# Spreading a row maximum over the partitions: by nine TensorE transposes, or by one and a trip through DRAM

## The chip, the core and the metric

The kernel runs on one core of a Trainium2 chip. The metric is the device time of one execution in microseconds (us). The engines are named as in the profile: PE is TensorE (PEld its weight loads), DVE VectorE, ACT ScalarE, POOL GpSimd, SP SyncE, which here only issues DMAs. L213 is line 213 of the kernel before.

## What is computed

Attention (batch 2, 8 heads, 576 positions, head size 64, rotary embedding) gives 1152 tokens of 512 numbers. A first mixture of 8 experts follows, weighted by a normalised table, and then a second mixture, in which every token goes to exactly one expert and no expert takes more than 144:

```python
N, D = x.shape                       # 1152, 512
E = w_gate.shape[1]                  # 8
cap = N // E                         # 144
logits = x @ w_gate
flat = logits.flatten()
order = np.argsort(-flat)
assigned = -np.ones(N, dtype=np.int64)
counts = np.zeros(E, dtype=np.int64)
for idx in order:
    tok, e = (int(idx) // E, int(idx) % E)
    if assigned[tok] >= 0 or counts[e] >= cap:
        continue
    assigned[tok] = e
    counts[e] += 1
out = np.zeros((N, D), dtype=np.float32)
for e in range(E):
    mask = assigned == e
    h = np.maximum(x[mask] @ w1[e], 0.0)
    out[mask] = h @ w2[e]
```

## The kernel before

Everything ahead of the second mixture is the same in both kernels. The second mixture (`moe2`) replaces the sorted walk by eight **phases**, each of which fills one expert. Tokens lie as 9 tiles of 128 partitions.

**A phase p**, p = 0 to 6. `prefer` (L205, L206) masks the experts that are full and takes each token's best logit, m, a [128, 9] tile. To compare every token with every other, each partition needs all 1152 best logits: the tile `mb`, [128, 9, 128]. `bcast` (L213) makes it with PE, nine transposes of one column of m spread over 128 columns, in three PSUM banks, and `bcopy` (L216) copies each bank to SBUF on ACT. `onehot` (L221 to L226) marks each token's best expert. `compare` on DVE (L245 to L248) and `above` on ACT (L237, L239) fill nine tables `cmp`, one for each tile j of the other token; ACT takes part of tables 5 to 8. `count` (L256) multiplies the tables with the marks on PE, in three groups of 27 matmuls, so that each token learns how many better ones want its expert. `assign`, `total`, `close` and `left` (L264 to L297) settle who is placed and which expert is now full.

Then expert p's tokens are collected: `select` and `place` (L309 to L319), `spread` (L326, L328), `index` (18 matmuls, L342), `address` (L348, L350), and `gather` (L360), two indirect DMAs on POOL's queue (xa, xb: 72 rows of ysc each), which end with a memset of `tick` (L364). ysc is the DRAM copy of the tokens; `save` (L1039) writes it tile by tile from SP, the last from ACT. `weights` loads the expert's weights on SP: four DMAs of 512 KB (`wlo`, L380) after a register load of the expert's number, and four (`whi`, L384) after a load of `tick`, that is, after the gather has been issued. Phase 7 needs no comparison.

**An expert p** turns the gathered rows (`tin`, L445 and L446; for expert 0 `turn` and `join`, L455 and L461, which add the part that never went to DRAM), runs 32 products into h (L471, ACT relu L474) and 32 into y (L481, ACT copy L484), turns y back (`tout`, L490, ACT L491) and scatters it (L496). Each product is two matmuls on the chip.

**What sets the order.** Phases and experts, and the last products of the first mixture (L769), are handed to `Plan`. It keeps a list of operations with what each needs and estimated durations per engine, and repeatedly emits the one that could start first; the products form its main line. Each engine then runs its instructions in that order. `HOLD` makes a phase's comparisons from table HOLD[p] on wait, on DVE, for the tick of the gather before (`hold`, L336): in phase 1 from table 1 on, in phase 2 from table 0 on. `mb`, `m` and the other phase tiles have two buffers; the PSUM bank PV has one.

Of the kernel before, what the change touches and what calls it, by code (L numbers as in the profile page):

```python
# [21 lines left out]
F32 = mybir.dt.float32  # L22
# [3 lines left out]
AF = mybir.ActivationFunctionType  # L26
# [5 lines left out]
N, D, E, F = 1152, 512, 8, 1024  # L32
# [3 lines left out]
NT = N // 128  # L36
# [6 lines left out]
@with_exitstack  # L43
def tile_attention_moe_moe2(
    ctx: ExitStack,
    tc: tile.TileContext,
    q: bass.AP,
    k: bass.AP,
    v: bass.AP,
    wg1: bass.AP,  # L50
    w1: bass.AP,
    w2: bass.AP,
    wg2t: bass.AP,
    w1b: bass.AP,
    w2b: bass.AP,
    rope: bass.AP,
    rt: bass.AP,
    out: bass.AP,
    dbg=None,
):  # L60
    nc = tc.nc
    ctx.enter_context(tc.manual_schedule())
    consts = ctx.enter_context(tc.tile_pool(name="consts", bufs=1))
    lp = ctx.enter_context(tc.tile_pool(name="big", bufs=1, side="right"))
    xst = ExitStack()
    xp = xst.enter_context(tc.tile_pool(name="xp", bufs=1, side="right"))

    ident = consts.tile([128, 128], F32, name="ident")
    make_identity(nc, ident)

    xH = xp.tile([128, KT, N], F32R, name="xH")
    xL = xp.tile([128, KT, N], F32R, name="xL")

    lg = consts.tile([128, NT, E], F32, name="lg")
    dram = ctx.enter_context(tc.tile_pool(name="dram", bufs=1, space=bass.MemoryType.DRAM))
    ysc = dram.tile([N + 1, D], F32, name="ysc")
    ps = ctx.enter_context(tc.tile_pool(name="ps", bufs=2, space=PSUM))
    sst = ExitStack()
    pss = sst.enter_context(tc.tile_pool(name="pss", bufs=2, space=PSUM))
    if dbg is not None and "xT" in dbg:  # L80
        with xst, sst:
            attention(tc, nc, ps, pss, lp, q, k, v, rope, ident, xH, xL, None)
            nc.sync.dma_start(dbg["xT"][0], xH.bitcast(F32))
            nc.sync.dma_start(dbg["xT"][1], xL.bitcast(F32))
        return
    m1 = Moe1(tc, nc, ctx, ps, sst, lp, wg1, w1, w2, wg2t, rt, ident, xH, xL, lg, ysc)
    attention(tc, nc, ps, pss, lp, q, k, v, rope, ident, xH, xL, m1)
    m1.rest()
    if dbg is not None and "acc" in dbg:
        m1.dbg = dbg["acc"]  # L90
        nc.sync.dma_start(dbg["lg"], lg)
    xst.close()
    moe2(tc, nc, ctx, ps, m1, w1b, w2b, ident, lg, ysc, out)


TINY = 2.0 ** -120
# [67 lines left out]


CFG = dict(CG=3, NCMP=6, HA=20, LEAD=8, FILL=0)
JA = 5
MAIN, HOLD, AT = 0.715, {1: 1, 2: 0}, (33, 34)


def moe2(tc, nc, ctx, ps, m1, w1b, w2b, ident, lg, ysc, out):
    BIG = 3.0e38
    FAR = 1.0e6
    if True:
        two = ctx.enter_context(tc.tile_pool(name="m2b", bufs=2, side="right"))
# [13 lines left out]
        def tb(x):  # L189
            return x.unsqueeze(1).to_broadcast([128, NT, E])  # L190
# [3 lines left out]
        def phase(p):  # L194
            d = {}
            S_[p] = d
            last = p == E - 1

            def prefer():
                lm = two.tile([128, NT, E], F32, name="lm") if p else None  # L200
                m = two.tile([128, NT], F32, name="m")
                if p == 0:
                    lm = lg
                else:
                    V.tensor_tensor(lm, lg, tb(pen), op=OP.add)  # L205
                V.tensor_reduce(m, lm, axis=AX.X, op=OP.max)  # L206
                d["lm"], d["m"] = lm, m
                d["mb"] = two.tile([128, NT, 128], F32, name="mb")

            def bcast(c):  # L210
                d["pm", c] = pm = ps.tile([128, 512], F32, name="T", bufs=3)[:, 0:384].rearrange("p (t c) -> p t c", t=3)
                for t in range(3):
                    nc.tensor.transpose(pm[:, t], d["m"][:, c * 3 + t:c * 3 + t + 1].to_broadcast([128, 128]), ident)  # L213
# [27 lines left out]
            def compare(j):  # L241
                g = table(j)
                mj = d["m"][:, j:j + 1]
                if 0 < j < JA:
                    V.tensor_scalar(g[:, :j], d["mb"][:, :j], mj, None, op0=OP.is_lt)  # L245
# [142 lines left out]
            def op(name, deps, segs, f, *a):  # L388
                plan.add((name, p), [x if isinstance(x, tuple) else (x, p) for x in deps], segs,
                         lambda: f(*a))  # L390

            if not last:
                op("m", [("close", p - 1), ("left", p - 1)] + ([("at", p)] if p == 1 else []) if p else [("fold", 1)], [("DVE", 0.5, 0.15)], prefer)
                for c in range(3):
                    op(f"bc{c}", ["m"], [("PE", 0.33, 0.2)], bcast, c)
                    op(f"mb{c}", [f"bc{c}"], [("ACT", 0.37, 0.1)], bcopy, c)
                op("oh", ["m"] + ([("ad", p - 1)] if p in HOLD else []), [("DVE", 1.35, 0.1)], onehot)
                mb = ["mb0", "mb1", "mb2"]
                for j in range(JA, NT):
                    op(f"sg{j}", mb[:(j - 1) // 3 + 1], [("ACT", 0.19 + 0.107 * j, 0.1)], above, j, 0)  # L400
                    op(f"re{j}", [f"sg{j}"], [("ACT", 0.1 + 0.107 * j, 0.1)], above, j, 1)
                for j in range(NT):
                    op(f"cmp{j}", mb + (["hold"] if j >= HOLD.get(p, NT) else []), [("DVE", 1.06 if j < JA else 0.88 - 0.067 * (j - 1), 0.15)], compare, j)
                cg = CFG["CG"]
                if p in HOLD:
                    op("hold", [("ga", p - 1)], [("DVE", 0.1, 0.1)], hold)
                js = [list(range(j, min(j + cg, NT))) for j in range(0, NT, cg)]
                for n, g in enumerate(js):
                    op(f"cnt{n}", ["oh"] + [f"cmp{j}" for j in g] + [f"re{j}" for j in g if j >= JA] + (["cnt0"] if n else [("add1", 0)] if p == 1 else []),
                       [("PE", 0.23 * len(g), 0.2)], count, g)  # L410
                op("as", [f"cnt{n}" for n in range(len(js))], [("DVE", 0.8, 0.1)], assign)
                op("tot", ["as"], [("PE", 0.04, 0.2)], total)
                op("left", ["as"], [("DVE", 0.4, 0.1)], left)
                op("close", ["tot"], [("DVE", 1.1, 0.1)], close)
                op("sel", ["close", "left"], [("DVE", 0.6, 0.1)], select)
            else:
                op("sel", [("sel", p - 1), ("left", p - 1)], [("DVE", 1.3, 0.1)], select)
            op("wlo", ["sel" if last else "close"] + ([("yend", p - 3)] if p > 2 else []) + ([("whi", p - 1)] if p else []) + ([("t", 35)] if p == 1 else []),
               [("SP", 0.3, 0), ("DMA", 7.0 if p else 3.5, 2.0)], weights, 0, 4 if p else 2)
            op("pl", ["sel"], [("PE", 0.2, 0.2)], place)  # L420
            op("spr", ["pl"], [("DVE", 1.65, 0.1)], spread)
# [105 lines left out]
        for n, (f, save) in enumerate(m1.tail()):  # L527
# [10 lines left out]
            elif save:  # L538
                t, evac = save
# [13 lines left out]
        for p in range(E):  # L553
            phase(p)
            expert(p)
# [1066 lines left out]
```

## Time and profile before

| | us |
|---|---|
| median of three runs | 1123.04 (1122.49 to 1125.29) |
| the profiled execution | 1122.86 |
| its span, first to last instruction | 1121.1 |
| PE busy in the span | 1102.6 (98%) |
| DVE, POOL, ACT busy | 745.7, 438.6, 412.8 |

The second mixture's phases begin at about 917 us of the span and end at 1044; experts 0 to 3 run beside them, experts 4 to 7 after. Busy time is read by stretch, since the stages have different limits; a wait is read from the idle time of an engine and from what ended it.

### The profile page before, as it was taken

How to read it: one execution, taken by the hardware profiler on the slowest of the kernel's cores; microseconds unless marked ns; L12 is line 12 of the kernel's file. 1: busy time of each engine (PE TensorE's matmuls, PEld its weight loads, DVE VectorE, ACT ScalarE, POOL GpSimd, SP SyncE). 2: the span in 40 equal slices, each digit the busy share in tenths (PEclk: the TensorE clock that was granted, in tenths of full speed). 3: DMA queues.
4: the chain of work that ended last, by engine and by line, in shares of the span. 5: the costliest groups of instructions: out<-in, count | busy, mean ns of one | idle time of the engine just before them, and what ended most of it. 6: DMA issues, size and time to landing. Idle time of an engine off the chain costs nothing.

```text
span 1121.1 us, 20946 instructions
## 1 busy us (share of the span) xinstructions
PE 1102.6 (98%) x8171; PEld 962.0 (86%) x8171; DVE 745.7 (67%) x1688; ACT 412.8 (37%) x903; POOL 438.6 (39%) x449
## 2 busy tenths in 40 slices
PE   7999999999999999999999999999999999999997
PEld 4666678998888888888888889989889888999997
DVE  5777733564777777777777777666678887778200
ACT  5777742143223223222223223232331133566222
POOL 6778353065434335434334534345310000234211
PEclk8999999999999999999999999999999999999999
DMA  5332322001233222432322422112130004879920
GB/s 130 79 74 51 99 82 76 1 1 57 82 98 94 85 86 88 125 98 75 95 85 75 126 92 66 38 39 74 39 141 11 30 1 165 277 250 354 292 75 22
DMA packets 105458, 107.22 MB, mean 96 GB/s; under 512 B 35600, under 2 KB 68752, under 8 KB 105232
## 3 DMA queue, kind: packets, MB, share of 16 engines
q1 hardware_dynamic: 102528, 100.40, 28.6%
q0 software_dynamic: 2048, 4.72, 1.4%
q8 instruction: 64, 1.05, 0.4%
q10 hardware_dynamic: 784, 0.77, 0.2%
q14 instruction: 34, 0.28, 0.1%
HBM read 98.85 MB, written 4.72 MB: 92 GB/s over the span
## 4 chain that ended last, share of the span: by engine, by line
PE 88%; DVE 3%; DMA 3%; issue 2%; ACT 2%; POOL 1%; SPq 1%; POOLq 0%; DVEq 0%; ACTq 0%
PE Y L1001 23%; PE T L939 21%; PE T L750 9%; PE Y L769 8%; PE Y L471 5%; PE Y L481 5%; PE T L1454 3%; PE S L1415 3%; PE T L1382 3%; DMA fr<-in_moe_w 2%; PE T L256 1%; DVE acc L1003 1%; PE PV L1382 1%; DVE v L952 1%; PE PV L1454 1%
## 5 line engine op out<-in xcount | busy, mean ns | idle before, releaser
L939 PE MATMUL T<-xH,wa 128*128 128x256 f32 (+1 forms) x576 | 137.8, 294 | 0.9 <-ACT v L959 0.8
L939 PEld LDWEIGHTS T<-big,wb 128*128 128x128 f32 x864 | 125.7, 188 | 10.8 <-DVE v L952 1.8
L939 PE MATMUL T<-big,wb 128*128 128x256 f32 (+1 forms) x864 | 133.0, 296 | 0.0
L952 DVE TENSOR_TENSOR v<-T,v 128x256 f32<-128x256 f32 (+1 forms) x240 | 108.1, 450 | 37.4 <-PE T L939 34.5
L1003 DVE SCALAR_TENSOR_TENSOR acc<-Y,pw,acc 128x512 f32<-128x512 f32 x168 | 122.5, 742 | 1.5 <-PE Y L1001 0.4
L939 PEld LDWEIGHTS T<-xH,wa 128*128 128x128 f32 x576 | 100.0, 188 | 9.5 <-ACT v L959 3.8
L750 PE MATMUL T<-xH,wa 128*128 128x384 f32 x336 | 92.9, 337 | 0.0
L848 POOL TENSOR_TENSOR wa<-wraw,wa 128x512 fp32r<-128x512 f32 (+1 forms) x48 | 48.8, 1018 | 106.3 <-ACT wa L847 106.3
L945 ACT ACTIVATE hhA<-v 128x256 fp32r<-128x256 f32 x72 | 30.1, 418 | 149.3 <-DVE v L952 149.3
L939 PE MATMUL T<-xL,wa 128*128 128x256 f32 (+1 forms) x288 | 84.5, 293 | 0.0
L945 ACT ACTIVATE hhB<-v 128x320 fp32r<-128x320 f32 x72 | 34.0, 472 | 136.5 <-DVE v L952 136.5
L946 DVE SCALAR_TENSOR_TENSOR hlB<-v,hhB 128x320 fp32r<-128x320 f32 x72 | 57.0, 792 | 38.7 <-ACT hhB L945 38.7
L1001 PE MATMUL Y<-wa,hhB 128*128 128x512 f32 x240 | 75.2, 395 | 0.0
L1001 PE MATMUL Y<-wb,hhB 128*128 128x512 f32 x240 | 75.2, 395 | 0.0
L1073 DVE SCALAR_TENSOR_TENSOR fr<-fr,fc 128x512 f32<-128x512 f32 x64 | 52.5, 820 | 33.6 <-DMA fr<-in_moe_w 33.6
L946 DVE SCALAR_TENSOR_TENSOR hlA<-v,hhA 128x256 fp32r<-128x256 f32 x72 | 51.1, 709 | 35.3 <-ACT hhA L945 35.3
L867 POOL TENSOR_TENSOR wb<-wraw,wb 128x512 fp32r<-128x512 f32 x24 | 30.6, 1299 | 101.9 <-ACT wb L866 101.9
L867 POOL TENSOR_TENSOR wa<-wraw,wa 128x512 fp32r<-128x512 f32 x24 | 30.6, 1294 | 99.1 <-ACT wa L866 99.1
L769 PE MATMUL Y<-wb,hh 128*128 128x512 f32 x216 | 68.4, 398 | 0.0
L750 PEld LDWEIGHTS T<-xH,wa 128*128 128x128 f32 x336 | 61.3, 188 | 2.9 <-issue 0.9
L1424 DVE TENSOR_REDUCE negmax<-S 128x1 f32<-128x576 f32 x72 | 53.8, 748 | 15.0 <-PE S L1415 14.1
L1001 PE MATMUL Y<-wa,hhA 128*128 128x512 f32 x192 | 59.9, 393 | 0.0
(343 smaller groups left out, 2729.1 us busy)
## 6 DMA issues: line engine op xcount, KB each, us to landing
wraw<-in_moe_w SPq DMA_DIRECT2D x52, 512.0 KB, 5.4
fr<-in_moe_w SPq DMA_DIRECT2D x64, 256.0 KB, 5.1
wraw<-in_moe_w SPq DMA_DIRECT2D x48, 256.0 KB, 3.2
big<-in_moe_w SPq DMA_DIRECT2D x20, 512.0 KB, 7.9
wa<-in_moe_w SPq DMA_DIRECT2D x18, 512.0 KB, 5.2
wb<-in_moe_w SPq DMA_DIRECT2D x14, 512.0 KB, 7.6
fc<-in_moe_w_gate SPq DMA_DIRECT2D x9, 256.0 KB, 3.5
t1q<-t1q SPq DMA_DIRECT2D x14, 160.0 KB, 2.8
```

The lines of the kernel that those rows point to most:

```text
L471: nc.tensor.matmul(Z["ph"][:, f % 2], d["wa"][kt // 2][:, kt % 2, f * 128:(f + 1) * 128], Z["xg", p][:, kt], start=(kt == 0), stop=(kt == ...
L481: nc.tensor.matmul(Z["py"][:, b % 2], d["wb"][f // 4][:, f % 4, b * 128:(b + 1) * 128], Z["h", p][:, f], start=(f == 0), stop=(f == FB - 1))
L750: nc.tensor.matmul(p[:, :CH], w[:, wi, kt, (fb % 2) * 128:(fb % 2) * 128 + 128], x[:, kt, o], start=(n == 0), stop=(n == 11))
L769: nc.tensor.matmul(self.Y[c][t], a[:, o], w[:, wi, fb % 2], start=(fb == 0 and n == 0), stop=(fb == FB - 1 and n == 2))
L867: G.tensor_tensor(d["W"][:, 1, h], r[:, 2 + h], d["W"][:, 0, h].bitcast(F32), op=OP.subtract)
L939: nc.tensor.matmul(bank[:, 0:n], d[t][:, ww, b, r * 128:(r + 1) * 128], x(xw, r), start=(first and i == 0), stop=(i == 5), skip_group_chec ...
L945: A.activation(HH[:, f, o], src, AF.Relu)
L946: V.scalar_tensor_tensor(HL[:, f, o], src, 0.0, HH[:, f, o].bitcast(F32), op0=OP.max, op1=OP.subtract)
L952: V.tensor_tensor(o, bank[:, 0:n], x, op=OP.add)
L1001: nc.tensor.matmul(y, h[:, f, o], w[:, ww, f], start=(f == 0 and z == 0), stop=(f == 1 and z == 2))
L1003: V.scalar_tensor_tensor(self.at(t), y, self.pw[:, t, e:e + 1], self.at(t), op0=OP.mult, op1=OP.add)
L1424: V.tensor_reduce(m[0:n], SS[P, i][0:n, :, :288], axis=AX.XY, op=OP.max, negate=True)
```

## The change

From phase 1 on (`VIA = 1`) the nine transposes and three copies go. Instead `turn_m` transposes the whole m at once into a [9, 128] tile (PE, into the bank PV) and copies it to SBUF (ACT), `send_m` writes its 4.6 KB to a DRAM tile from ACT's queue, and `spread_m` reads them back from SP's queue into every partition of mb (576 KB). The plan gets a time for each, `HOLD[1]` goes from 1 to 0, and `wlo` of phases 1 to 5 is made to come after `spread_m` of the next phase.

```diff
-    moe2(tc, nc, ctx, ps, m1, w1b, w2b, ident, lg, ysc, out)
+    moe2(tc, nc, ctx, ps, m1, w1b, w2b, ident, lg, ysc, dram, out)
...
-JA = 5
-MAIN, HOLD, AT = 0.715, {1: 1, 2: 0}, (33, 34)
+JA, VIA = 5, 1
+MAIN, HOLD, AT = 0.715, {1: 0, 2: 0}, (33, 34)
...
+            def turn_m():
+                pt = ps.tile([128, 512], F32, name="PV", bufs=1)[0:NT, 0:128]
+                nc.tensor.transpose(pt, d["m"], ident)
+                d["mt"] = two.tile([NT, 128], F32, name="mt")
+                nc.scalar.activation(d["mt"], pt, AF.Copy)
+
+            def send_m():
+                d["mr"] = dram.tile([NT, 128], F32, name=f"mr{p}")
+                nc.scalar.dma_start(d["mr"], d["mt"])
+
+            def spread_m():
+                nc.sync.dma_start(d["mb"].rearrange("p t c -> p (t c)"),
+                                  d["mr"].rearrange("t c -> (t c)").partition_broadcast(128))
...
-                for c in range(3):
-                    op(f"bc{c}", ["m"], [("PE", 0.33, 0.2)], bcast, c)
-                    op(f"mb{c}", [f"bc{c}"], [("ACT", 0.37, 0.1)], bcopy, c)
+                if p < VIA:
+                    for c in range(3):
+                        op(f"bc{c}", ["m"], [("PE", 0.33, 0.2)], bcast, c)
+                        op(f"mb{c}", [f"bc{c}"], [("ACT", 0.37, 0.1)], bcopy, c)
+                else:
+                    op("ms", ["m"], [("PE", 0.12, 0.2), ("ACT", 0.25, 0.1)], turn_m)
+                    op("mw", ["ms"], [("ACT", 0.06, 0.0)], send_m)
+                    op("ml", ["mw"], [("NONE", 0.0, 2.2)], lambda: None)
+                    op("mi", ["ml"], [("SP", 0.1, 0.0)], spread_m)
+                    for c in range(3):
+                        op(f"mb{c}", ["mi"], [("NONE", 0.0, 3.4)], lambda: None)
...
-            op("wlo", ["sel" if last else "close"] + ([("yend", p - 3)] if p > 2 else []) + ([("whi", p - 1)] if p else []) + ([("t", 35)] if p == 1 else []),
+            op("wlo", ["sel" if last else "close"] + ([("yend", p - 3)] if p > 2 else []) + ([("whi", p - 1)] if p else []) + ([("t", 35)] if p == 1 else []) + ([("mi", p + 1)] if max(VIA - 1, 1) <= p < E - 2 else []),
```

The lines of `moe2` move by 14, and from the list of a phase's operations on by 22: bcast L213 becomes L227, the new transpose is L212, its copy L214, the write L218, the read L221, index L356, h L493 and y L503.

On PE, the turn of m in a later phase. Before, in phase 4, it falls among expert 2's products y (h, wb and wraw are their operands), behind the last matmul of `place`:

```order
L319 MATMUL PV<-selb,ones_b 128x1
L481 MATMUL Y<-h,wb 128x144
L481 MATMUL Y<-h,wraw 128x144
L213 MATMUL T<-ident,m 128x128 x9
L481 MATMUL Y<-h,wraw 128x144 x2
```

In the changed kernel it falls among an expert's products h (xg and wb are their operands), and so in each of phases 3 to 6:

```order
L333 MATMUL PV<-selb,ones_b 128x1
L493 MATMUL Y<-xg,wb 128x144 x2
L212 MATMUL PV<-ident,m 9x128
L493 MATMUL Y<-xg,wb 128x144 x6
L356 LDWEIGHTS hot
```

Nine transposes became one, and the phase stands later against the experts; counted on in the same order, 39 products and the index lie between this turn and the first counts, and 64 products, the three count groups and expert transposes between it and the next turn.

On ACT, in phase 5. Before, three copies fill mb and the comparisons follow at once:

```order
L474 ACTIVATE h<-Y 128x288 x3
L216 ACTIVATE mb<-T 128x384 x3
L237 ACTIVATE cmp_11279<-mb,m 128x640
L237 ACTIVATE cmp_11282<-mb,m 128x768
L474 ACTIVATE h<-Y 128x288
```

Now:

```order
L496 ACTIVATE h<-Y 128x288
L214 ACTIVATE mt<-PV 9x128
L496 ACTIVATE h<-Y 128x288
L218 DMA mr_11305<-mt 9x128
L496 ACTIVATE h<-Y 128x288 x2
L251 ACTIVATE cmp_11386<-mb,m 128x640
```

One relu of h stands between the copy of the turned row and the issue of its write, and two more ahead of the first comparison.

On SP, between the last weight loads of one expert (`whi`) and the first of the next (`wlo`); the ISA rows set registers. Before:

```order
L384 DMA wb<-in_moe_w 128x2x512
L384 ISA
L384 DMA wb<-in_moe_w 128x2x512
L368 TENSOR_LOAD ei
L368 ISA x2
L380 ISA
L380 DMA wb<-in_moe_w 128x2x512
```

Now:

```order
L398 DMA wb<-in_moe_w 128x2x512
L398 ISA
L398 DMA wb<-in_moe_w 128x2x512
L221 DMA mb<-mr_10605 128x1152
L382 TENSOR_LOAD ei
L382 ISA x2
L394 ISA
L394 DMA wb<-in_moe_w 128x2x512
```

The read of mb for phase 3, which waits for the write of the row, now stands ahead of the register load and of expert 2's first four weight loads.

## Rows read from the trace of the kernel before

**Rows 1.** The page, parts 1 and 2: busy time; PE's granted clock in tenths.

```profile
PE 1102.6 (98%) x8171; PEld 962.0 (86%) x8171; DVE 745.7 (67%) x1688; ACT 412.8 (37%) x903; POOL 438.6 (39%) x449
...
PEclk8999999999999999999999999999999999999999
```

**Rows 2.** Stretches: length, busy PE, PEld, DVE, ACT, POOL; PEclk, DMA share, GB/s.

```profile
960.00:970.00 10.00, 10.00 (x128) 9.93 (x128) 7.35 (x23) 6.01 (x9) 1.48 (x3) 1.00 0.99 326
1030.00:1040.00 10.00, 10.00 (x148) 9.88 (x145) 7.22 (x38) 4.08 (x7) 5.06 (x3) 1.00 0.94 314
```

**Rows 3.** Chain that ended last, in order of time: start, us, engine, tile, line, count.

```profile
956.33 0.98 PE T L213 x9
...
958.05 0.60 PE PV L342 x18
...
974.86 0.44 PE Y L490 x4
...
982.25 0.66 PE T L256 x27
...
1047.48 6.13 PE Y L471 x50
```

**Rows 4.** Timeline of PE at the first gather: start, us, instruction, [idle before <-releaser].

```profile
944.67 0.87 PE L769 MATMUL Y<-big,wraw 128*128 128x512 f32 x3
945.69 1.11 PE L455 MATMUL Y<-ident,xa 72*128 72x72 f32 x8 [0.15 <-DMA xa<-ysc,ix]
```

**Rows 5.** Timelines of SP's queue and of POOL, same columns: seventh ysc write, first gather.

```profile
935.96 0.40 SPq L1039 DMA_DIRECT2D ysc<-acc  x1
...
942.34 1.15 POOL L360 DMA_INDIRECT xa<-ysc,ix  x1 [10.30 <-ACT cmp L237]
```

**Rows 6.** DMA issues by window or whole span: count, KB each, us to landing.

```profile
ysc<-acc SPq DMA_DIRECT2D x1, 256.0 KB, 5.2
...
ysc<-pen SPq DMA_DIRECT2D x1, 2.0 KB, 2.2
...
ysc<-acl SPq DMA_DIRECT2D x1, 256.0 KB, 2.0
ysc<-acl ACTq DMA_DIRECT2D x1, 256.0 KB, 5.5
...
wa<-in_moe_w SPq DMA_DIRECT2D x1, 512.0 KB, 3.8
...
fc<-in_moe_w_gate SPq DMA_DIRECT2D x9, 256.0 KB, 3.5
...
g<-in_moe_w_gate SPq DMA_DIRECT2D x1, 2048.0 KB, 7.5
...
big<-in_moe_w SPq DMA_DIRECT2D x1, 512.0 KB, 9.3
```

**Rows 7.** Timeline of DVE, columns as in rows 4: the tick, comparisons of phase 3.

```profile
944.87 0.14 DVE L336 COPY rest<-tick 1x1 int32<-1x1 int32 x1 [3.42 <-POOL tick L364]
...
978.06 0.75 DVE L247 TENSOR_SCALAR cmp<-mb,m 128x1024 bf16<-128x1024 f32 x1 [0.97 <-ACT mb L216]
...
979.26 0.39 DVE L245 TENSOR_SCALAR cmp<-mb,m 128x128 bf16<-128x128 f32 x1
...
984.07 0.34 DVE L247 TENSOR_SCALAR cmp<-mb,m 128x256 bf16<-128x256 f32 x1
...
987.16 0.23 DVE L264 TENSOR_TENSOR ok<-T,rem 128x72 f32<-128x72 f32 x1 [1.77 <-PE T L256]
```

**Rows 8.** Timeline of POOL: gathers; then the tile xb: landing of seven second halves.

```profile
959.46 0.98 POOL L360 DMA_INDIRECT xa<-ysc,ix  x1 [6.28 <-DVE key L222]
...
996.33 5.68 POOL L360 DMA_INDIRECT xb<-ysc,ix  x1 [0.31 <-PE Y L481]
...
1027.02 6.76 POOL L360 DMA_INDIRECT xa<-ysc,ix  x1 [0.30 <-issue]
...
DMA to landing us min/median/max: 3.2/7.3/8.0
```

More of the change, by code (lines that the diff above doesn't have):

```diff
@@ L166, with moe2 @@
 CFG = dict(CG=3, NCMP=6, HA=20, LEAD=8, FILL=0)
-JA = 5
-MAIN, HOLD, AT = 0.715, {1: 1, 2: 0}, (33, 34)
-def moe2(tc, nc, ctx, ps, m1, w1b, w2b, ident, lg, ysc, out):
+JA, VIA = 5, 1
+MAIN, HOLD, AT = 0.715, {1: 0, 2: 0}, (33, 34)
+def moe2(tc, nc, ctx, ps, m1, w1b, w2b, ident, lg, ysc, dram, out):
     BIG = 3.0e38
```

## The prediction

> **What bounds the kernel now.** First the page: TensorE (PE) is busy 98% of the span and its granted clock stands at the upper level (2.4 GHz) in all slices but the first [rows 1]. A mean over the span says nothing of the second mixture, so next the table of stretches: from 960 us on PE is busy for 10.00 of 10 us, and the DMA engines are nearly full beside it [rows 2]. The list of waits has no PE wait at all between 950 and 1063 us, and the chain of work that ended last runs there through PE alone, piece against piece [rows 3]. So in this stage whatever leaves PE's stream shortens the kernel, and whatever makes PE wait lengthens it one for one. There is one place before it where PE does wait: at the first gather [rows 4].
>
> The profiled execution took 1122.86 us, its span 1121.1, 0.18 below the median of 1123.04. I sum against 1122.86 and count no change in the 1.76 us outside the span.
>
> **What leaves PE.** Each of phases 1 to 6 loses nine transposes of 128 columns, 0.98 us together, 0.109 each [rows 3]. It gains one: the operand is 128x9 and the identity's 128 columns pass through it. The nearest row is the turn of y, four of 128 columns in 0.44 us, so 0.11 [rows 3]. Net 0.87 us a phase, 5.2 us for six. ScalarE's three copies of mb also go, but ScalarE is not the bound; the copy of 9x128 and the DMA issue take their place.
>
> **Phase 1's 0.87 is lost.** Its transposes stand ahead of the last 33 products of the first mixture. Those end at 945.54, and PE then waits until 945.69 for the gathered rows xa [rows 4]. The gather started at 942.34, after the write of ysc that SP issued at 935.96 had landed 5.2 us later, at 941.2 [rows 5, 6]. The issue of that write stays ahead of the new load on SP's queue, so the gather moves neither forward nor back. PE is there 0.87 earlier and waits 0.87 longer. That leaves 5 x 0.87 = 4.35.
>
> HOLD moves phase 1's first comparison behind the wait for the gather's tick at 944.87: about 0.9 us, as in phase 3 from its start at 978.06 to the next table's at 979.26, less two small operations of 0.3 [rows 7]. The last comparisons end some 1.8 us later (the 0.9, and as much for two sums of the last tile that now stand ahead of them), but the third group of counts is also put two products later and one more interruption is made. Following both orders from 945.69, I get PE 0.1 us later than before at the same amount of work: +0.1 (bounds 0 and 0.9, the comparison wholly hidden or wholly on the path).
>
> **What the round trip costs.** Phases no longer run ahead: in the new order each of phases 3 to 6 takes just one expert's time of PE. I count PE from the turn of m (the transpose of m, time 0). 39 products of two matmuls each, 0.245 a product [rows 3], and the index (0.60) come before the first counts: about 10.2 us. The first tin comes at 12.0 (one count group of 0.66 and four products later), the second counts at 12.8, and the turn of the next phase at 20.4. The data must keep up:
> - m turned 0.11, copied by about 0.55; the write stands behind one relu of h on ScalarE's queue, so it is issued at about 1.15.
> - The write, 4.6 KB. Nearest row: 2 KB to the same tensor landed in 2.2 us [rows 6]. From above, 5.5 us, a 256 KB write from the same queue while weights streamed [rows 6]. I take 2.2, since in the new order the last weights of the expert before should have left some microseconds earlier (about 5.2 MB a phase, from 3.4 us on, at the 326 GB/s of rows 2 is 16 us of 20.4): landed 3.35.
> - The read, 576 KB to all partitions, on SP: 512 KB of weights on an idle queue took 3.8, and two loads that spread one row, fc (256 KB) and g (2048 KB), took 3.5 and 7.5, between which 576 KB lies at 4.2 [rows 6]. From above 9.3, a weight load behind three others [rows 6]. I take 3.7 to 4.3: mb is there at 7.1 to 7.7 us.
> - Comparisons 0 to 5 end 5.7 us after mb: in phase 3 they began at 978.06 and the sixth ended at 984.07, less the same 0.3 [rows 7]. So 12.8 to 13.4, and PE wants the sixth 0.44 into the second counts, at 13.2. ScalarE's comparisons are due at the third counts and come in time.
>
> PE waits 0 to 0.3 us a phase, say 0.15. Phase 2 is looser (the write follows the copy at once). Four phases: +0.6. What is queued behind the wait: SP stands still until the row has landed, and behind it lie the register load and the first four weight loads of the expert before. They go out about 4.5 us after the turn; the products that want them start 14 us after it, and a load took 3.8 [rows 6]. That cover is 5 us thick.
>
> The Trainium skill's page "DMA: Bandwidth & Descriptors" (section "Anatomy of one DMA — SWDGE (gpsimd) path") gives a fit, for the GpSimd path, of 2.0 us and the bytes over 436 GB/s. By it write and read would be 2.0 and 3.35 us, an estimate from that page: mb at about 6.8 and no wait at the counts, so 0.6 us less. The rows differ: 512 KB would be 3.2 by the fit and took 3.8 at best.
>
> **What nearer gathers cost.** The new order also shortens each gather's lead. The index ends at 2.2, and in phase 1 the gather began 0.8 after it [rows 3, 8]; four small DVE operations now stand between, so 3.2. tin wants both halves at 12.0: 8.8 us. The second half is issued 1.3 us after the first and landed 7.3 us later at the median, 8.0 at most: 8.6 and 9.3 [rows 8]. Before, this was hidden by some 12 us more. PE waits 0 to 0.6 a phase; I take 0.2, five times: +1.0.
>
> **Sum.** 1122.86 - 5.2 + 0.87 + 0.1 + 0.6 + 1.0 = 1120.2 us.
>
> **The rivals.**
> 1. *Everything fits.* The round trip costs PE nothing, as a phase has slack I haven't seen; the time is 1122.86 - 4.35 = 1118.5. For it: in phases 2 and 3 before, PE came to the last counts after the comparisons (DVE waited 1.77 us for PE in rows 7). Against it: the new chain is as long as an expert's time.
> 2. *The round trip is slow, and the kernel gets slower.* Write and read fall into the stream of weights. If the write takes 5.5 instead of 2.2, mb is 3.3 us later and PE waits that long in each of phases 3 to 6, 2.5 in phase 2: 1122.86 - 4.25 + 15.7 = 1134.3; with half of that delay 1126.5. It breaks even at 0.85 us a phase, mb at 8.2, and is slower by more than 0.3% from 1.5 a phase on. For it: DMA share 0.94 to 0.99 [rows 2], and 5.5 against 2.0 for one and the same write under load and without [rows 6]. Against it: the mb read stands ahead of the weights on SP, and the weights of the expert before are done. The Trainium skill's same page, section "Latency and other measured facts", puts HBM's access latency at 0.2 us on average and 2 us at high load. That speaks for this rival; no run here shows the latency apart.
> 3. *A gather is held up on GpSimd.* Two of seven took 5.7 and 6.8 us to issue [rows 8]. In the second, at 1027.02, both halves were there 13.3 us after its start: PE would wait 4.5. One such: 1120.2 + 4.3 = 1124.5.
> 4. *It doesn't do what it says:* the transposes were not on the path. Rows 3 and the missing PE waits exclude it for phases 2 to 6.
>
> **How the numbers follow.** A measurement of this kernel can tell 0.3%, 3.4 us, from no change: faster is below 1119.7, slower above 1126.4. Forecast 0.62, with its terms at their bounds 1118.6 to 1123; about 0.25 of it lies below 1119.7. Rival 1: 0.15. Rival 2: 0.14, nearly all above 1126.4. Rival 3: 0.09. Faster 0.25 + 0.15 = 0.40, slower 0.14, same 0.46. The range takes in rival 1 and one held gather, and leaves out rival 2 and the ends: 1118.0 to 1124.6.
>
> **What would show it.** Right: a row of one transpose for m of about 0.11 us, six times; PE waiting about 1 us for xa at the first gather; write and read landing in about 2.2 and 4 us; PE waits of some tenths at counts and tin from phase 2 on, and the two experts without a phase at the end as long as now. Wrong: PE waits of over 0.85 us a phase at the counts (rival 2), none at all (rival 1), a first gather that starts earlier or later than 6.4 us after SP's issue of the seventh ysc write, or waits for the weights of an expert, which I have at zero.

## The result, and the profile after

| | before | changed |
|---|---|---|
| median of 15 executions | 1122.49 (1120.66 to 1126.23) | 1129.68 (1122.89 to 1136.52) |
| profiled execution | 1122.86 | 1129.68 |
| its span | 1121.1 | 1127.9 |

The ratio of the times is 1.0068, with an interval of 1.0055 to 1.008: slower by 7.2 us, where the prediction had 1120.2 and a range that ended at 1124.6. The profiled execution is longer by 6.8 us. The ratios here and below leave out three executions that were disturbed as a whole (two of f2_hold, one of h1_quiet), which the medians count.

The page, parts 1 and 2, answers to [rows 1]. PE is as busy as before, and in tenths its clock shows nothing either:

```profile
PE 1100.9 (98%) x8120; PEld 958.2 (85%) x8123; DVE 747.4 (66%) x1688; ACT 408.6 (36%) x891; POOL 425.8 (38%) x449
...
PEclk8999999999999999999999999999999999999999
```

PE's waits between 905 and 1128 us (waiting line, what ended it: us in total, times, longest) show it better. In the kernel before the whole list for this stage is 0.6 us:

```profile
PE Y L468 <- DMA xb<-ysc,ix: 6.4, 5, 3.5
PE Y L477 <- DMA xa<-ysc,ix: 1.7, 1, 1.7
PE Y L512 <- ACT y L506: 0.3, 1, 0.3
```

All but the last 0.3 us is waits for gathered rows; no wait for the counts and none for an expert's weights is among them. The largest is before expert 6. Timeline of PE (start, us, instruction, idle before it and what ended that), answering to [rows 4], first at the first gather, then at expert 6:

```profile
945.04 0.87 PE L791 MATMUL Y<-big,wraw 128*128 128x512 f32 x3
947.61 1.11 PE L477 MATMUL Y<-ident,xa 72*128 72x72 f32 x8 [1.69 <-DMA xa<-ysc,ix]
...
1072.02 6.29 PE L503 MATMUL Y<-h,big 128*128 128x144 f32 x50
1078.14 0.23 PE L467 MATMUL Y<-ident,xa 72*128 72x72 f32 x1
1081.87 0.28 PE L468 MATMUL Y<-ident,xb 72*128 72x72 f32 x1 [3.49 <-DMA xb<-ysc,ix]
```

Behind that wait stands a loss that no list of waits has. The table of stretches by one microsecond (length, busy PE, PEld, DVE, ACT, POOL, granted clock, DMA share, GB/s), columns as in [rows 2]:

```profile
1082.00:1083.00 1.00, 1.00 (x11) 1.00 (x12) 0.00 (x0) 0.41 (x1) 0.00 (x0) 1.00 1.01 277
1083.00:1084.00 1.00, 1.00 (x10) 1.00 (x9) 0.00 (x0) 0.41 (x1) 0.00 (x0) 0.74 1.06 363
1084.00:1085.00 1.00, 1.00 (x6) 1.00 (x5) 0.00 (x0) 0.00 (x0) 0.00 (x0) 0.50 1.04 387
1085.00:1086.00 1.00, 1.00 (x6) 1.00 (x5) 0.00 (x0) 0.41 (x1) 0.00 (x0) 0.50 1.10 395
1086.00:1087.00 1.00, 1.00 (x6) 0.84 (x6) 0.00 (x0) 0.00 (x0) 0.00 (x0) 0.55 0.99 367
1087.00:1088.00 1.00, 1.00 (x10) 0.99 (x9) 0.00 (x0) 0.59 (x1) 0.00 (x0) 1.00 1.07 393
```

PE is busy without a gap, but it does 6 matmuls a microsecond instead of 10 or 11: the granted clock is at 0.50, the lower level of 1.2 GHz, from 1083.5 to 1086.9. The missing clock adds up to 0.26 + 0.50 + 0.50 + 0.45 = 1.7 us.

**The bill of the profiled execution.** From PE's timeline I take the stretch from the first transpose of phase 0 to PE's last matmul, the gaps in it, and the missing clock; the rest is PE at work:

| kernel | stretch | gaps | missing clock | rest |
|---|---|---|---|---|
| before | 195.9 | 0.6 | 0 | 195.3 |
| changed | 201.4 | 8.6 | 1.7 | 191.1 |

PE does save 4.2 us net. It pays 8.0 in gaps and 1.7 in clock, +5.5 in all. A further 1.2 us lies ahead of the stretch, which begins at 919.6 and began at 918.4; the change does not touch that part, and over the profiled runs below its start varies from 915.2 to 919.6. Sum 6.7, measured 6.8.

That execution's time is the median of the 15, but its mean clock, 0.994, is above their median of 0.990 (0.996 over 18 executions of the kernel before). So many executions lose more to the clock than this trace shows, and those that take as long must lose less elsewhere.

### The profile page after: what moved, and what is told of

It reads as the page before. It is cut to its first block, busy times and chain, and to the rows that moved or that the text cites. A ratio compares the mean times of both kernels' runs of the same rounds, so it can differ in the third digit from the quotient of the medians.

```text
span 1127.9 us, 20855 instructions
## 1 busy us (share of the span) xinstructions
PE 1100.9 (98%) x8120; PEld 958.2 (85%) x8123; DVE 747.4 (66%) x1688; ACT 408.6 (36%) x891; POOL 425.8 (38%) x449
## 3 DMA queue, kind: packets, MB, share of 16 engines
q0 software_dynamic: 2048, 4.72, 1.5%
## 4 chain that ended last, share of the span: by engine, by line
PE 82%; DMA 7%; DVE 3%; issue 3%; POOL 2%; SPq 1%; ACT 1%; POOLq 0%; DVEq 0%; ACTq 0%
PE Y L1023 23%; PE T L961 22%; PE T L772 9%; PE Y L791 8%; DMA xb<-ysc,ix 4%; PE Y L493 4%; PE T L1476 3%; PE T L1404 2%; PE S L1437 2%; DMA fr<-in_moe_w 2%; PE Y L503 2%; PE T L270 1%; PE PV L1404 1%; PE PV L1476 1%; DVE acc L1025 1%
```

## Experiments

The table gives, for each kernel, the median, the ratio to the kernel before with its interval, and the bill of its profiled execution. Names are those of the headings below. The lead of a gather is the time from its issue to PE's first use of its rows; the lead theory of the expectations has the loss in leads that became too short, the round-trip theory in the trip through DRAM itself.

| kernel | median us | ratio | stretch | gaps | missing clock | rest |
|---|---|---|---|---|---|---|
| e1_none | 1125.92 | 1.0033 [1.0021, 1.0044] | 196.9 | 0.8 | 0 | 196.1 |
| e2_late | 1120.52 | 0.9984 [0.9973, 0.9994] | 195.8 | 0.8 | 1.7 | 193.3 |
| e3_from3 | 1126.44 | 1.0038 [1.0025, 1.0051] | 199.9 | 4.8 | 1.7 | 193.3 |
| f1_late_hold | 1118.20 | 0.9964 [0.9950, 0.9978] | 193.2 | 0.5 | 0 | 192.7 |
| g_via5_hold | 1120.57 | 0.9977 [0.9967, 0.9987] | 194.5 | 0.6 | 0 | 193.9 |
| g_via3_hold | 1124.35 | 1.0016 [1.0003, 1.0028] | 197.7 | 4.7 | 0 | 193.0 |
| f2_hold | 1127.57 | 1.0044 [1.0023, 1.0066] | 197.8 | 6.6 | 0 | 191.2 |
| f3_order | 1127.35 | 1.0047 [1.0030, 1.0065] | 201.6 | 4.2 | 1.7 | 195.7 |
| f4_lead2 | 1123.65 | 1.0016 [1.0003, 1.0030] | 198.6 | 3.1 | 5.1 | 190.4 |
| h2_again (the changed kernel) | 1130.03 | 1.0061 [1.0044, 1.0078] | 203.5 | 9.8 | 1.7 | 191.9 |

### How many phases go through DRAM: e1_none, e2_late, e3_from3

```
-JA, VIA = 5, 1
+JA, VIA = 5, 7      (e1_none; 4 in e2_late, 3 in e3_from3)
```

> No phase goes through DRAM; of the change only the HOLD of the first phase is left (before's transposes in all phases). Lead theory (the loss is that the phases no longer run ahead, so that each expert's gather is issued 7 us before its first transpose, where it was 10 to 33, and lands after TensorE gets there): 1122.5, as before, no wait of TensorE for xb over 0.3 us. Round-trip theory (each phase through DRAM costs 7.2 / 6 = 1.2 us of itself): 1122.5 too. HOLD theory (the earlier first gather disturbs what follows): 1127 to 1130.

> Only phases 4, 5 and 6 go through DRAM. Lead theory: the first phases run ahead as in the kernel before, and by the planner's own table every gather is issued 12.6 us or more before its first transpose; so TensorE waits under 0.5 us in all for xb, the clock stays whole, and three phases' saving of 0.87 us is left: 1119.9 (1119.3 to 1121). Round-trip theory: 3 x 1.2 us more than before, 1126.1.

> Phases 3 to 6 go through DRAM. Lead theory: the shortest leads in the planner's table are 10.8 and 11.1 us (experts 2 and 3), the others 14 or more; four savings of 0.87 us and at most 1 us of waits: 1119.0 to 1120.5. Round-trip theory: 4 x 1.2 us more, 1127.3.

e2_late came out as the lead theory had it, and against the round-trip theory: three phases through DRAM make the kernel faster than before, PE waits 0.2 us for rows, and the rest falls by 2.8 us against e1_none, 0.93 a phase. So neither the saving nor the round trip of these three phases is at fault. e1_none and e3_from3 missed both theories. e1_none, where only HOLD differs from the kernel before, is 3.3 us slower by the medians; its profiled run, the fastest of its seven at 1122.31, does not show where. e3_from3 has 4.8 us of gaps, 0.5 of them at the gathers; g_via3_hold below shows what they are.

### The same with the old HOLD: f1_late_hold, g_via5_hold, g_via3_hold

```
-MAIN, HOLD, AT = 0.715, {1: 0, 2: 0}, (33, 34)
+MAIN, HOLD, AT = 0.715, {1: 1, 2: 0}, (33, 34)
```

> Phases 4 to 6 through DRAM as in e2_late, and the HOLD of the kernel before (phase 1: one column's comparison may go ahead of the first gather). If HOLD alone made e1_none 3 us slower than before (by comparisons that come late to the counts, and a clock that falls behind them at 950 us), the same is won here: 1117.5 (1116.5 to 1119). If e1_none's 3 us came from elsewhere: 1120.5, as e2_late.

> Phases 5 and 6 through DRAM, HOLD as before. Lead theory: leads of 18 us and more but for the first experts', as before; two savings of 0.87 us and no cost: 1119.5 to 1120.5, between the kernel before and f1_late_hold.

> Phases 3 to 6 through DRAM, HOLD as before (e3_from3 with f1_late_hold's HOLD). By leads alone (10.8 us and more) a fourth saving is added to f1_late_hold's 1118.2: 1117 to 1118.5. By e3_from3's profile, where TensorE waits 2.1 us in all at the turn for a bank of PSUM that VectorE has yet to read, and 1.5 us at one expert's first products: 1120 to 1124.

With VIA = 4, f1_late_hold is faster than both kernels: 1118.2 us. All of PE's waits over 0.2 us in its stage, same columns as above:

```profile
PE Y L512 <- ACT y L506: 0.3, 1, 0.3
PE Y L477 <- DMA xb<-ysc,ix: 0.2, 1, 0.2
```

Its rest is 2.6 us below that of the kernel before, 3 x 0.87 exactly as the prediction priced a phase; two phases (g_via5_hold) give 1.4. By the medians f1_late_hold gains 3.7 us on the kernel before, about 1 more than its bill shows; where that comes from is open. The old HOLD is worth 2.3 us against e2_late. Where HOLD's cost goes is only half shown: e2_late and e3_from3, with the new HOLD and phase 1 still on the transposes, ran at half clock for 3.4 us at 951 to 956 in their profiled runs, e1_none did not, and the three runs here and the kernel before did not either.

With a fourth phase the gain is gone, as e3_from3's profile had said (1124.35 us, just above the range expected from it). PE's timeline of g_via3_hold shows one of two such waits, and DVE's timeline what PE waits for:

```profile
975.89 0.28 PE L212 MATMUL PV<-ident,m 128*9 128x128 f32 x1 [1.07 <-DVE pos L340]
```

```profile
974.46 0.23 DVE L235 TENSOR_TENSOR key<-lm,m 128x72 f32<-128x72 f32 x1
...
975.53 0.23 DVE L240 TENSOR_TENSOR oh<-key,u 128x72 bf16<-128x72 f32 x1
975.68 0.16 DVE L340 SCALAR_TENSOR_TENSOR pos<-sel,PV 128x9 f32<-128x9 f32 x1
```

The one transpose writes the bank PV, of which there is one. The placing of the phase before has just written to it, and DVE reads that (pos) only after the five small operations of the new phase's one-hot. So the new instruction brings a wait of its own, for a bank, which the old transposes into T did not have. 1.7 us more in that run are two waits at products of an expert that the profile does not attribute.

### Order without the round trip, and the round trip with more lead: f3_order, f4_lead2

```
 def turn_m():                                # f3_order
+    for c in range(3):
+        bcast(c)
+        bcopy(c)
 ...
 def send_m() / spread_m():
+    pass
```

```
-CFG = dict(CG=3, NCMP=6, HA=20, LEAD=8, FILL=0)
+CFG = dict(CG=3, NCMP=6, HA=20, LEAD=2, FILL=0)      # f4_lead2
```

> The changed kernel's order of instructions on every engine (the planner is told of the same round trip), but without the round trip: the nine transposes and three copies of the kernel before stand where the one transpose stands, and no row is written or read. Lead theory: the gathers stand where they stood, 7 us ahead of their use, so TensorE still waits 5 to 9 us for them; 6 x 0.87 = 5.2 us of transposes come back: 1133 to 1136. Traffic theory (the read of 576 KB makes gathers and weights late): the waits go, and 1122 to 1126 is left.

> The changed kernel, all six round trips in it; only the mark from which TensorE may turn an expert's rows stands 2 matmuls ahead of the expert, not 8. In the planner's table the gathers then stand 8.8 to 27 us ahead of their use (6.3 to 8.8 for experts 0 to 6 in the changed kernel), and its end is 1.9 us later. Lead theory: the waits for xb (6.4 us) and the clock's fall (1.7 us) go, 1.9 us come: 1121.5 to 1125. Round-trip or traffic theory: 1129.7 + 1.9, 1130 to 1132.

The order alone is enough for most of the loss. f3_order reads and writes no row, does all the old transposes (rest 195.7, about as before), and still waits 3.6 us for xb, 2.3 of it before expert 6, with half clock for 3.4 us behind it:

```profile
PE Y L465 <- DMA xb<-ysc,ix: 3.6, 3, 2.3
```

Its 1127.35 lies below what I expected, since 0.87 us of transposes in each phase fill part of the waits: none is left for experts 1 to 3, and for expert 6 it is 2.27 where it was 3.49. f4_lead2 keeps all six round trips and moves only the place from which an expert's rows may be turned; by that the phases get ahead again, the second halves of the gathers are issued 9.1, 11.9, 14.2, 15.1, 15.8 and 13.0 us ahead of their first use for experts 1 to 6 (changed kernel: 8.7, 7.8, 8.0, 7.8, 7.7 and 10.0, each with the wait in it), and no wait for xb remains. 6 us are won, as the lead theory said. What keeps it above f1_late_hold in the two profiled runs is the clock, 5.1 us, and 2.6 us more of gaps, against 2.3 us less work. Stretches of f4_lead2 at the first gather, columns as above:

```profile
943.00:944.00 1.00, 0.89 (x4) 0.38 (x2) 0.00 (x0) 0.00 (x0) 0.99 (x2) 1.00 0.96 359
944.00:945.00 1.00, 0.00 (x0) 0.00 (x0) 0.84 (x3) 0.70 (x1) 0.00 (x0) 1.00 0.75 240
945.00:946.00 1.00, 0.70 (x6) 0.70 (x7) 1.00 (x4) 1.00 (x3) 0.00 (x0) 1.00 0.56 139
946.00:947.00 1.00, 1.00 (x10) 0.95 (x9) 1.00 (x4) 1.00 (x2) 0.00 (x0) 0.93 0.52 150
947.00:948.00 1.00, 1.00 (x6) 1.00 (x6) 1.00 (x4) 1.00 (x2) 0.00 (x0) 0.50 0.99 354
...
957.00:958.00 1.00, 1.00 (x10) 1.00 (x9) 0.75 (x4) 0.00 (x0) 0.31 (x1) 0.95 0.04 16
```

PE waited 1.41 us for the first gather, until 945.3, and from 946.9 to 957.1 it ran at the lower level: a wait of 1.4 us and 5.1 us of missing clock. In the changed kernel's profiled run the same wait, 1.69 us, was followed by no fall. So much the same wait was followed by a fall in one profiled run and not in another.

### The wait at the first gather filled, and HOLD alone: g1_fill, g2_lead2_fill, f2_hold

```
 def turn(h):
+    for _ in range(0 if h else 11):          # 9, and LEAD=2, in g2_lead2_fill
+        nc.tensor.matmul(Z["pt"][1].rearrange("p k c -> p (k c)"), ones_b,
+                         d["hot"].rearrange("p t c -> p (t c)")[:, 0:2 * CAP],
+                         start=True, stop=True, skip_group_check=True)
```

> The changed kernel, with 11 matmuls of 288 columns ahead of the first turn of expert 0's gathered rows, written to a bank that is written over at once; they leave nothing out and take about 1.3 us of the 1.7 us in which TensorE waited there. If that wait is what halves the clock at 946 to 957 us in many runs (f4_lead2's profiled run shows the fall 1.6 us after the wait's end, the changed kernel's profiled run doesn't): the first turn starts when it did, the clock stays whole there, and the median falls by 2 to 4 us, to 1125.5 to 1128. If the fall has another cause: 1129 to 1130, or up to 1.3 us more where the fillers come on top.

> f4_lead2 with 9 such matmuls (1.1 us of its wait of 1.4 us). Its waits for the later experts' rows are gone already, so this wait and the 11 us at half clock behind it are what is left: 1119 to 1121.5 if the wait makes the fall, 1123 to 1125 if not.

> The changed kernel with HOLD as before. HOLD theory: 3 us back, 1126.5. Lead theory: phase 1's comparisons wait for the row from DRAM anyway, so HOLD holds nothing up there; 1129 to 1131, gather 0 up to 0.9 us later.

Filling that wait won nothing: g1_fill 1131.37 us, ratio 1.0069 [1.0052, 1.0086]; g2_lead2_fill 1124.94, 1.0014 [1.0002, 1.0026]. In both the wait at the first gather shrank to 0.4 us, and neither profile has half clock there. But in g1_fill the same 8.6 us of gaps stand elsewhere (5.9 for xb and 1.0 for xa at later experts, 0.9 for the bank PV), with half clock at 971 to 978 and 1084 to 1087. In g2_lead2_fill 5.0 us of gaps are spread over the bank PV, counts and products. So the theory that the first gather's wait is what is wrong in the typical execution fell. f2_hold, 1.0044 [1.0023, 1.0066], overlaps with the changed kernel's two intervals; what HOLD does there is not settled.

### What makes a gather late: e4_free_w, h1_quiet, h3_quiet_lo, h4_quiet_all, h2_again

e4_free_w takes away the rule that an expert's first weights stand behind the next phase's read of the row on SP:

```
-... + ([("mi", p + 1)] if max(VIA - 1, 1) <= p < E - 2 else []),
+...,
```

> All six phases go through DRAM, but SyncE issues an expert's first weights at once and not behind the next phase's read of the row, so 4 to 5 us earlier, ahead of the gather and not beside it; TensorE's order and the leads are those of the changed kernel. If the weights beside the gather make it late: waits for xb fall from 6.4 us to under 2, but the row's read stands behind 2 MB of weights, 5 us by the rate of 387 GB/s in the trace, and counts wait 2 to 5 us in five phases: 1130 to 1145. If the lead alone decides: waits for xb stay at 5 to 8 us, and the time is 1129 plus what the counts wait. If the round trip has 5 us to spare: below 1126.

1160.62 us, ratio 1.0335 [1.0313, 1.0357], far beyond what I expected. PE's waits:

```profile
PE T L270 <- DVE cmp L262: 19.6, 15, 3.2
PE Y L468 <- DMA xb<-ysc,ix: 2.5, 1, 2.5
PE Y L477 <- DMA xa<-ysc,ix: 1.5, 1, 1.5
PE PV L212 <- DVE pos L340: 1.4, 4, 0.5
```

The gathers are better off (2.5 us where it was 6.4; they land in 6.1 us at the median and not 7.8), in part because the counts now wait and PE comes to the rows 12.3 to 12.8 us after the issue of xb for experts 1 to 5. ACT issued the write of one row at 986.20, SP could issue its read only at 990.97: in phases 2 to 6, behind 2 MB of weights, the read followed the write of 4.5 KB by 4.8 to 5.7 us, where in the changed kernel it followed by 1.3 to 1.4. The clock costs as much again: it is at half in seven stretches between 943 and 1117 us, and of the 41.7 us by which the stretch is longer than in the kernel before, missing clock is 25.6 and gaps 25.2. So the round trip fits only where the weights stand back for it, and standing back is what puts them beside the gather.

The last three cut traffic and leave the order: of each 512 KB of an expert's weights (experts 1 to 7) only 64 KB are loaded, and the products read the loaded part again, with as many matmuls. For either half that takes 12.8 MB off the 110.8 MB that the DMA engines move. These kernels leave out most of the weights, so they serve only to time the gathers.

```
-nc.sync.dma_start(d["wa"][k][:, :, o], w1b[..., k * 256:(k + 1) * 256, o] ...)
+a = 1 if p else 2                            # h3_quiet_lo, first halves (whi likewise in h1_quiet)
+o = slice(o.start, o.start + 128) if p else o
+nc.sync.dma_start(d["wa"][k][:, 0:a, o], w1b[..., k * 256:k * 256 + a * 128, o] ...)
```

> The changed kernel with the second halves of the weights of experts 1 to 7 loaded only in part (64 KB of each 512 KB, and the second products read the loaded part again and again, with as many matmuls as before): 14 MB of reads less beside the gathers, the order of everything as in the changed kernel. If the weights beside a gather set its landing: xb lands in 3 to 6 us, not 7.8, so the lead of 7.7 us is enough, waits for xb fall from 6.4 us to under 1.5, the clock stays whole behind them: 1121 to 1124. If a gather takes 7 to 8 us by itself: waits and time as in the changed kernel, 1128 to 1131.

> The changed kernel itself beside h1_quiet, for a second profiled execution. If its loss is waits for gathers plus a clock halved behind some of them: 1127 to 1131 again, waits for xa and xb of 5 to 10 us in all, and each stretch of half clock begins within a few us of a wait of 1 us or more. If the clock falls without such waits, the clock's loss is not a consequence of the late gathers.

> The changed kernel with the first halves of the weights of experts 1 to 7 loaded only in part (64 KB of each 512 KB; the first products read the loaded part again and again). These are the 2 MB that SyncE issues in the same microsecond as the gather; the second halves, issued behind it, are whole, the other way about than in h1_quiet. If the first halves beside it set the gather's landing: xb lands in 3 to 5.5 us, waits for xb fall under 1 us in all, and the wait of 1.7 us at the first gather is what is left: 1121 to 1124. If the landing stays near 7.8 us: 1127 to 1131, as h1_quiet.

> Both halves cut to 64 KB of each 512 KB for experts 1 to 7: next to no traffic is left beside a gather but the row's read. If traffic sets the landing: xb lands in 3 to 4 us as the first gather's second half does (3.2), no waits for xb, 1120 to 1123. If a gather of 72 rows needs 7 to 8 us by itself in this order: 1127 to 1131, and the traffic theory is out.

Landing of the eight second halves, from the tile xb (minimum, median, maximum), in the changed kernel, h1_quiet, h3_quiet_lo and h4_quiet_all:

```profile
DMA to landing us min/median/max: 3.2/7.8/9.9
```

```profile
DMA to landing us min/median/max: 3.1/7.8/8.2
```

```profile
DMA to landing us min/median/max: 3.1/3.8/7.9
```

```profile
DMA to landing us min/median/max: 3.3/3.7/4.3
```

With the second halves of the weights cut (h1_quiet) the median landing is the same, and experts 1 to 5 wait 0.73 to 0.89 us each; only the wait at expert 6 is gone. Its clock is at half behind the first gather (944 to 951 us) and 2 us after expert 2's wait (995 to 999). 1129.0 us, 1.0036 [1.0014, 1.0058]. With the first halves cut (h3_quiet_lo) a gather lands in 3.8 us, PE's waits for xb are 0.7 us in all, and the time is 1122.02, 1.0001 [0.9989, 1.0014]; with both (h4_quiet_all) 3.7 us, no wait for xb, 1120.58, 0.9978 [0.9966, 0.9989]. So it is the 2 MB that SP starts to issue in the same microsecond as the gather that make it land 4 us later for experts 1 to 5. Experts 6 and 7 still take 7.1 and 7.9 us in h3_quiet_lo and 3.6 and 3.5 in h4_quiet_all: there the second halves do it too. h4_quiet_all still waits 2.5 us at the first gather and then runs at half clock from 944.9 to 955.1, which takes 5.1 us.

h2_again repeats the bill: waits of 6.0 us for xb, 1.9 for xa and 1.4 for the bank PV, and half clock for 3.4 us at 1081 to 1085, right behind a wait of 2.18 us for expert 6's rows. Its six waits for xb, experts 1 to 6, are 1.00, 1.18, 0.53, 0.83, 0.30 and 2.18 us.

## Why the prediction was wrong, point by point

**The bound, and what leaves PE: right.** PE is the bound of the stage, and one transpose of 0.11 us stands where nine stood. From the chain of waits of the changed kernel, answering to [rows 3], and the expert-6 gather further down the same chain:

```profile
1044.95 0.11 PE PV L212
...
1071.90 9.92 DMA xb<-ysc,ix
```

The transposes alone saved what was forecast: counted from each start to the next, without gaps and missing clock, those of m took 6.7 us before and 1.5 now (0.9 in phase 0, 0.6 for the six new ones). But PE's work in all fell by 4.2 us in the one profile and 3.4 in the other. The largest part of the difference is in the 72 turns of gathered rows, which took 5.7 us before, 6.9 in both profiles, and 5.7 again in h3_quiet_lo, where the gathers are on time: between turns that follow each other it is 0.06 us from start to start, while one that is followed by a wait takes its whole 0.23. So late gathers cost about 1.1 us that the list of waits does not show. The three phases of f1_late_hold saved 2.6, the full 0.87 each.

**Phase 1's 0.87 at the first gather: right in kind, short in size.** PE waits 1.69 us where it waited 0.15 and then 0.16 [rows 4]. I had about 1. PE was there 0.8 us earlier, counted from phase 0's first transpose (26.3 and 27.1), the gather began 0.3 later by the same count (6.6 us after SP's issue of the seventh ysc write, where the prediction had 6.4) and landed in 3.7 us, not 3.3.

**HOLD: not settled.** I had +0.1 with 0.9 at most. By itself it costs 3.3 us (e1_none) and beside three round trips 2.3 (f1_late_hold against e2_late); with all six it could be anything from nothing to that.

**The round trip: right, even too dear.** PE did not wait for the counts at all, where I had 0.6. The read landed in 3.3 to 4.3 us (I took 3.7 to 4.3), and in phases 2 to 6 it followed the write by 1.3 to 1.4 (I took 2.2 for the write). ACT's timeline, then SP's:

```profile
1045.65 0.27 ACTq L218 DMA_DIRECT2D mr<-mt  x1
```

```profile
1047.02 0.34 SPq L221 DMA_DIRECT2D mb<-mr  x1
```

In phase 1, beside a 256 KB write of ysc and two weight loads, the read followed by 4.6 us, and PE did not wait for that either. An estimate by the fit on the Trainium skill's page "DMA: Bandwidth & Descriptors" (section "Anatomy of one DMA — SWDGE (gpsimd) path") gave 3.35 for the read, which is at the lower end of the rows, and 2.0 for the write, which the rows do not bear out; added up with the prediction's own 1.15, these two give mb at 6.5 us, not at the 6.8 that stands there. Rival 1 was right about the round trip, but not about the time. Rival 2 is out for this kernel: slower it was, but not by the waits to which the prediction gave that outcome. It is what e4_free_w became, by the mechanism that it named: there the read followed the write, behind weights, by 4.8 to 5.7 us, near the 5.5 of [rows 6]. Nor did rival 3 occur: every gather was issued in 0.95 to 1.15 us.

**What nearer gathers cost: this step failed, +1.0 against 6.4 (6.0 in h2_again).** It set a lead of 7.5 us from the issue of xb against a landing of 7.3 at the median and 8.0 at most. For experts 2 to 5 the lead came out (7.4 to 7.7 us), xb landed in 7.7 to 7.9 us, and the waits of this profile, 0.11, 0.54, 0.34 and 0.31, lie within the 0.6 at most, if above the 0.2 that I took. Expert 1 cost 1.69 (its xb landed in 8.7 us), and expert 6, which I had not looked at apart, 3.49. In h2_again the middle is worse (up to 1.18 at expert 2) and expert 6 better (2.18). So the margin was too thin for every expert, and thinnest at the end. The end of the chain differs: the last phase has no maxima of its own, so phases 6 and 7 place together, no read of a row holds the weights back any more, and both experts' go out in one burst around the gather. POOL's timeline, then SP's:

```profile
1070.62 0.98 POOL L374 DMA_INDIRECT xa<-ysc,ix  x1 [4.93 <-issue]
1071.90 0.96 POOL L374 DMA_INDIRECT xb<-ysc,ix  x1 [0.30 <-issue]
```

```profile
1065.08 2.59 SPq L394 DMA_DIRECT2D wa<-in_moe_w  x4
1070.62 0.95 SPq L398 DMA_DIRECT2D wa<-in_moe_w  x2
1071.83 0.94 SPq L398 DMA_DIRECT2D big<-in_moe_w  x2
1073.63 0.38 SPq L394 DMA_DIRECT2D big<-in_moe_w  x1
1074.26 0.73 SPq L394 DMA_DIRECT2D wraw<-in_moe_w  x1
1075.19 0.61 SPq L394 DMA_DIRECT2D big<-in_moe_w  x1
1076.01 1.69 SPq L394 DMA_DIRECT2D wraw<-in_moe_w  x1
```

Twelve loads of 512 KB leave SP within 12.6 us, the DMA engines are full (share 0.99 to 1.10 from 1082 us in the table above), and the xb issued in their midst lands after 9.9 us. PE wants it 6.5 us after its issue. The four gathers that POOL issues there in a row are not enough by themselves: in h4_quiet_all, with the weights cut, these two second halves land in 3.6 and 3.5 us. The expectation that "the two experts without a phase at the end" stay as they were is the sentence that missed it.

The prediction had the other half of it in its own numbers: weight loads "about 4.5 us after the turn", and gathers at 3.2 and 4.5. It used the first for SP and the second for GpSimd and did not put them beside each other. In phase 5 the loads begin 3.3 us after the turn, the halves of the gather 3.5 and 4.8 us after it. What one costs the other is what h3_quiet_lo prices: 4 us on the gathers of experts 1 to 5. With these on time the kernel takes 1122.0 us and not 1129.7, with all on time (h4_quiet_all) 1120.6.

**The clock: no term at all.** I read the granted clock as whole from [rows 1] and counted every wait at its own length. In the changed kernel a wait of 3.49 us is followed by 1.7 us of missing clock. Over the executions the mean clock is 0.990 (and 0.992 in h2_again's) against 0.996 (0.995) for the kernel before: times the span of 1128 us, an estimate of 3.4 to 6.8 us of the 7.2, and at most that, since the clock is also at half for the last microseconds of every profiled span, behind PE's last matmul. Among the 15 executions the longest, 1136.52 us, has a clock of 0.986 and the shortest, 1122.89, of 0.997. They spread over 13.6 us, where the kernel before spread over 5.6; in h2_again's the spread was 7.2, no more than the 8.7 of the kernel before beside it. Where it falls in executions that were not profiled is open; in the profiled ones it is behind expert 6's wait (the changed kernel, h2_again, f3_order, g1_fill; not f2_hold, where that wait was 1.53 us), behind expert 1's in g1_fill (1.96 us) and near expert 2's in h1_quiet (0.73 us), behind the first gather's (f4_lead2, h1_quiet, h4_quiet_all; not the changed kernel, h2_again, f2_hold or h3_quiet_lo), and in e2_late and e3_from3 behind small gaps.

Put as a sum, the bill of the profiled execution is 1122.86 - 4.2 (PE's work) + 1.4 (first gather) + 6.4 (xb) + 0.2 (other gaps) + 1.7 (clock) + 1.2 (ahead of the stage) = 1129.6. That is a balance of measured terms and no test of them; what it shows is which terms the prediction had too small, the gathers and the clock.

## What to carry to other kernels

When a change takes work off the bound engine and puts a longer latency into the chain that feeds it, ask how far that chain ran ahead before, and give the latency only to the steps that have the lead to spare: here phases 4 to 6, with the old HOLD, for 1118.2 us, where all six with the new one gave 1129.7. Check the first and the last round of a pipelined order by themselves, since the holds that shape the middle rounds are missing there. And put the issue times of all queues on one axis: a gather needed in 7.5 us is on time alone and late beside 2 MB of weights.

## What was not expected of the hardware

- Half a gather (72 rows; 147 KB, by the page's 4.72 MB on GpSimd's queue over 32 transfers) landed in 3.8 us at the median with the loads beside it cut to an eighth, and in 7.8 with 2 MB of weights that SP began to issue in the same microsecond (h3_quiet_lo and the changed kernel). The Trainium skill's page "DMA: Bandwidth & Descriptors" (section "SWDGE vs HWDGE vs iDMA") says that the DMA engines take turns between the queues of the two kinds; an estimate by that, with both halves' 295 KB and as much of weights at the 387 GB/s of the stretch from 1084 us, is 0.8 us more than alone, and the rows show 4.
- From the issue of a write of 4.5 KB to that of the read that waits for it were 1.3 to 1.4 us in phases 2 to 6 of the changed kernel, 4.6 in its phase 1, beside a 256 KB write and two loads of 512 KB, and 4.8 to 5.7 behind 2 MB of weights (e4_free_w).
- The granted clock fell to its lower level behind a wait of 1.41 us and stayed there for 10.2 us, with PE busy all the time (f4_lead2); behind a wait of 1.69 us it did not fall (the changed kernel); and in e2_late it fell at 951 us for 3.4 us with no wait over 0.21 us ahead of it, PE having done turns of rows, counts of 8 columns, joins and three products since 943.6.
